# Squares of k from the third chunk on, instead of from the fourth

## The chip, the cores and the metric

The kernel runs on one core of one Trainium2 chip. The metric is the device time of one execution in microseconds (us). Several runs are made and their median is given; a profile is taken of one execution.

## The reference

A retention layer in its parallel form is followed by a feed-forward block, all in float32.

```python
# q, k, v: (8, 8, 576, 64)
scores = q @ k.T / sqrt(64)
Dmat[i, j] = gamma[h] ** (i - j) if i >= j else 0      # gamma[h] = 1 - 2 ** (-5 - h)
x = (scores * Dmat) @ v            # -> (8 * 576, 512) = (4608, 512)
h = x @ w_in                       # (512, 2048)
g = h * erf(softplus(h))
out = g @ w_out                    # (2048, 512)
```

The weights come as float64 and are rounded on the chip to float32.

## The kernel before, in words

**Pieces and chunks.** The 4608 tokens are cut into 36 pieces of 128 (`pieces`, L108). Four full pieces of batch b, four of batch b + 1, and a ninth made of the two tails of 64 tokens each; then the next two batches. So pieces 8, 17, 26 and 35 have two parts. Four pieces make a chunk (PC = 4), nine chunks the whole. Chunk 2, the third, is pieces 8 to 11.

**A piece of attention** has three steps (`stages`, L430). `transposes(i)` (L311) makes qT and kT, with the head dimension on the partitions. `scores(i)` (L337) multiplies them on TensorE (PE) into two PSUM tiles s, and VectorE (DVE) masks them into sT (L348). `outputs(i)` (L350) multiplies sT with v and qT with the state of the earlier pieces into two PSUM tiles o; for a piece of one part it also multiplies k with v (L384), for the state of the pieces behind it. DVE scales o into x, and POOL or DVE makes the new state (L423). A piece with two parts makes no state, so it does not use k by rows outside `transposes`.

**Two ways to a transpose.** By rows: `load_rows` (L136) brings q or k with the tokens on the partitions, in two loads of 128 KB (256 bytes in a row); PE transposes four times against an identity (L328) into a PSUM tile pt_q or pt_k, and ScalarE (ACT) copies it to qT or kT (L330, L334). By squares: `load_squares` (L123) brings the same numbers so that 32x32 blocks already lie where they belong; DVE then transposes inside the blocks, straight to qT or kT (L322), and PE and ACT have no part in it. Such a load is four DMAs of 112 KB for a full piece (896 bytes in a row) and eight of 48 KB for one with two parts. Squares hold each token's neighbours too, so 448 KB move instead of 256 KB. They have two buffers each (tags "qs" and "ks"); rows of k and v have four.

**Which way a piece goes.** Pieces below SQUARES = 8 go by rows. From piece 8 on q goes by squares (L153 to L156). k goes by squares from SQUARES_K = 12 on (L157); below that by rows. From 12 on, k by rows is loaded as well where the piece has one part, for L384 (L159). `transposes(i)` takes whichever is there (L317).

**Order of the work.** It is written out by hand. All DMAs that matter here are issued by SyncE (SP) in program order: `transposes(i)` ends with the loads of q, and of squares of k, of piece i + 2 (L335), and `outputs(i)` with those of k and v by rows of piece i + 3 (L426). Behind and between them SP also issues the weights (`load_weights`, L228), a second part of the constants (L733) and the stores of finished chunks of x (`store_x`, L460). The string at L723 orders the first chunk: "a" is the next step of attention, "p" four products of the first chunk of the feed-forward block, "w" a load of weights, a digit so many steps of rounding weights. Pieces 8 to 11 come behind that string, in `firsts[1].plain()` (L745, the second chunk of the feed-forward block) and in the blocks after it (from L754); their loads are issued earlier, from the end of the string on. Between these PE runs products p, pe, pg (L546) and a, e (L600). DVE rounds weights there too (L255 to L268), multiplies t by s (L569) and makes sums of w_out and w_in (L204, L214).

Of the kernel before, what the change touches and what calls it, by code (L numbers as in the profile page):

```python
# [54 lines left out]
def kernel(  # L55
# [45 lines left out]
    def flat(ap):  # L101
        return ap.rearrange("p h d -> p (h d)")
# [5 lines left out]
    pieces = []  # L108
# [3 lines left out]
    PC = TCH // P  # L112
# [4 lines left out]


    SQUARES = 2 * PC
    SQUARES_K = 3 * PC  # L120
    SQ = 32

    def load_squares(i, name, src):  # L123
        t = raw.tile([P, NP, P * D // SQ], FP32, tag=name + "s", name=f"raw_{name}s", bufs=2)
        for b, s0, n, r0 in pieces[i]:
            m = n // SQ * D
            for part in range(P // SQ):
                e, d0 = part // 2, part % 2 * SQ
                tokens = src[b, e * NP : (e + 1) * NP, s0 : s0 + n, :].rearrange("p (r a) d -> r p (a d)", r=SQ)
                at = r0 // SQ * D  # L130
                nc.sync.dma_start(  # L131
                    out=t[part * SQ : (part + 1) * SQ, :, at : at + m - SQ], in_=tokens[:, :, d0 : d0 + m - SQ]
                )
        return t

    def load_rows(i, name, src, bufs):  # L136
        if name == "q":
            t = raw.tile([P, NP, P * D // SQ], FP32, tag="qs", name="raw_q", bufs=bufs)
            t = t.rearrange("p a x -> p (a x)")[:, : H * D].rearrange("p (h d) -> p h d", h=H)
        else:  # L140
            t = raw.tile([P, H, D], FP32, tag=name, name=f"raw_{name}", bufs=bufs)
        for b, s0, n, r0 in pieces[i]:
            for e in range(2):
                heads = src[b, e * NP : (e + 1) * NP, s0 : s0 + n, :]
                nc.sync.dma_start(out=t[r0 : r0 + n, e::2, :], in_=heads.rearrange("h p d -> p h d"))  # L145
        return t

    def load(i, names="qkv"):
        if i < len(pieces):
            t = loaded.setdefault(i, {})  # L150
            for name in names:
                src = {"q": q, "k": k, "v": v}[name]
                if name == "q" and i < SQUARES:  # L153
                    t["q"] = load_rows(i, "q", q, 2)
                elif name == "q":
                    t["qs"] = load_squares(i, "q", q)  # L156
                    if i >= SQUARES_K:  # L157
                        t["ks"] = load_squares(i, "k", k)
                elif name == "v" or i < SQUARES_K or len(pieces[i]) == 1:  # L159
                    t[name] = load_rows(i, name, src, 4)  # L160

    load(0)
    cst = cpool.tile([P, CONST_COLS], FP32, name="cst")
    nc.sync.dma_start(out=cst[:, :CONST_FIRST], in_=consts[:, :CONST_FIRST])
# [4 lines left out]
    gq, gq2 = (g.rearrange("p (a i) -> p a i", a=NP) for g in (gq, gq2))  # L169
    gp = gp.unsqueeze(2).to_broadcast([P, NP, D])  # L170
    load(1)


# [128 lines left out]
    def weigh_values(i):  # L302


        if i < len(pieces) and i not in weighed:
            weighed.add(i)
            t = (loaded.get(i) or live[i])["v"]
            by = gk if len(pieces[i]) == 1 else gk2
            nc.gpsimd.tensor_tensor(out=t, in0=t, in1=by.unsqueeze(2).to_broadcast([P, H, D]), op=ALU.mult)

    def transposes(i):  # L311
        t = live[i] = loaded.pop(i)
        if i < SQUARES:
            weigh_values(i)
        for name in "qk":
            tT = t[name + "T"] = att.tile([P, NP, P], FP32, tag=name + "T", name=name + "T")
            if name + "s" in t:  # L317
                for _, _, n, r0 in pieces[i]:
                    a = r0 // SQ * D
                    squares = t[name + "s"][:, :, a : a + n // SQ * D].rearrange("p h (a d) -> p h a d", d=D)  # L320
                    order = "p h (a r) -> p h a r" if name == "q" else "p h (r a) -> p h a r"
                    nc.vector.transpose(  # L322
                        out=tT[:, :, r0 : r0 + n].rearrange(order, r=SQ), in_=squares[:, :, :, :SQ]
                    )
            else:
                pt = ps_at.tile([P, NP, P], FP32, tag="at", name=f"pt_{name}")
                for p in range(NP):
                    nc.tensor.transpose(pt[:, p, :], flat(t[name][:, 2 * p : 2 * p + 2, :]), ident)  # L328
                if name == "q":
                    nc.scalar.copy(  # L330
                        out=tT.rearrange("p h (a r) -> p h a r", r=SQ), in_=pt.rearrange("p h (r a) -> p h a r", r=SQ)
                    )
                else:
                    nc.scalar.copy(out=tT, in_=pt)  # L334
        load(i + 2, "q")  # L335
# [14 lines left out]
    def outputs(i):  # L350
# [76 lines left out]
        if i + 1 >= SQUARES:  # L427
            weigh_values(i + 1)

    stages = [(transposes, 0), (scores, 0)]  # L430
    for i in range(len(pieces)):
        stages += [(transposes, i + 1), (outputs, i), (scores, i + 1)]
        if i in (PC + 1, 2 * PC - 1):
            stages[-3:-1] = stages[-2], stages[-3]
# [397 lines left out]
```

## Time and profile before

| | |
|---|---|
| median of 3 runs | 1027.74 us (1027.37 to 1028.41) |
| the profiled execution's own time | 1027.74 us |
| its span | 1026.0 us |
| PE busy | 1017.5 us, 99% |
| DVE busy | 669.1 us, 65% |
| ACT busy | 390.4 us, 38% |
| POOL busy | 123.7 us, 12% |
| DMA | 165.76 MB, mean 162 GB/s |
| granted clock of TensorE | 0.999 |

The span runs from the first to the last instruction of the profiled execution; its own time is measured around it. "Busy" is the time in which an engine has at least one instruction running. A timeline line gives the start, the duration of the merged group, engine, line, operation, what is written from what, partitions and sizes, and the number of instructions merged. Buffer numbers are left out, so kT is the kT of any piece. SPq stands for SP's queue of instructions, which issues DMAs; a DMA lands some time after its issue. Pieces are told apart by their order in time: in the profile PE starts the scores of piece 8 at 64.77 us, of 9 at 73.84, of 10 at 82.44 and of 11 at 92.64.

### The profile page before, as it was taken

Reading aid. Unit: us, or ns where it says so; the run is one execution under the profiler, and the core shown is the slowest. Engines: PE = TensorE matmul, PEld = TensorE weight load, DVE = VectorE, ACT = ScalarE, POOL = GpSimd, SP = SyncE. Lnnn points to the kernel's source line nnn. Section 1 sums busy time; section 2 is a strip of 40 time slices with the busy share of each in tenths; the row PEclk is TensorE's granted clock in tenths of the full one; section 3 lists DMA queues with packets and bytes.
Section 4 is the critical chain, followed back from the end, with each engine's and each line's share of the span. In section 5 each row is a group of like instructions: output and inputs, shape, how many; then the busy total and the mean of one; then the engine's idle time right before and its main releaser. Section 6 shows DMA issues by size and latency. Waiting matters only on the chain.

```text
span 1026.0 us, 15946 instructions
## 1 busy us (share of the span) xinstructions
PE 1017.5 (99%) x6346; PEld 876.1 (85%) x6346; DVE 669.1 (65%) x1054; ACT 390.4 (38%) x481; POOL 123.7 (12%) x122
## 2 busy tenths in 40 slices
PE   9999999999999999999999999999999999999998
PEld 8778888888888888888888888888888888888887
DVE  3868777877976656656666666666567655555555
ACT  2254134233234444434343444444433333333332
POOL 2143112122312110010001001000100000000000
PEclk9999999999999999999999999999999999999999
DMA  9999889979984344544444345444333334444333
GB/s 197 191 241 194 224 194 221 251 155 248 242 187 161 120 150 145 168 158 163 156 150 163 123 146 160 167 144 144 144 124 124 123 131 126 131 136 133 124 91 115
DMA packets 146986, 165.76 MB, mean 162 GB/s; under 512 B 97376, under 2 KB 121568, under 8 KB 138848
## 3 DMA queue, kind: packets, MB, share of 16 engines
q1 hardware_dynamic: 145904, 163.96, 56.5%
q8 instruction: 50, 0.82, 0.3%
q10 hardware_dynamic: 1008, 0.79, 0.3%
q14 instruction: 24, 0.20, 0.1%
HBM read 117.52 MB, written 47.19 MB: 161 GB/s over the span
## 4 chain that ended last, share of the span: by engine, by line
PE 89%; DMA 5%; DVE 3%; SPq 3%; issue 1%; POOL 0%; DVEq 0%; POOLq 0%
PE a L600 23%; PE a L492 22%; PE g L600 11%; PE g L492 11%; PE e L600 6%; PE e L492 5%; PE s L343 3%; PE o L361 2%; DMA raw_qs<-in_q_dram 1%; PE p L546 1%; SPq L145 1%; PE o L384 1%; PE o L372 1%; DMA raw_k<-in_k_dram 1%; SPq L131 1%; DMA raw_ks<-in_k_dram 1%
## 5 line engine op out<-in xcount | busy, mean ns | idle before, releaser
L492 PE MATMUL a<-x,wa 128*128 128x256 f32 x1088 | 258.3, 380 | 0.0
L492 PEld LDWEIGHTS a<-x,wa 128*128 128x128 f32 x1088 | 205.7, 190 | 28.5
L600 PE MATMUL a<-wb,s 128*128 128x256 f32 x864 | 205.7, 381 | 0.0
L600 PEld LDWEIGHTS a<-wb,s 128*128 128x128 f32 x864 | 162.9, 190 | 23.6 <-ACT o L614 0.7
L99 DVE TENSOR_TENSOR t<-g,t 128x512 f32<-128x512 f32 x68 | 46.9, 690 | 150.3 <-ACT t L522 113.1
L492 PE MATMUL g<-x,wa 128*128 128x256 f32 x544 | 129.2, 380 | 0.0
L492 PEld LDWEIGHTS g<-x,wa 128*128 128x128 f32 x544 | 102.8, 190 | 14.4
L99 DVE TENSOR_TENSOR o<-a,o 128x512 f32<-128x512 f32 x108 | 74.2, 687 | 49.3 <-PE a L600 49.3
L517 ACT COPY t<-a 128x512 f32<-128x512 f32 x34 | 19.9, 586 | 188.2 <-PE a L492 188.2
L99 DVE TENSOR_TENSOR t<-t,s 128x1024 f32<-128x1024 f32 x72 | 89.6, 1285 | 0.0
L561 ACT ACTIVATE s<-t 128x1024 f32<-128x1024 f32 x72 | 72.1, 1049 | 27.8 <-DVE t L99 27.8
L270 POOL TENSOR_TENSOR wraw<-wraw 128x512 f32<-128x512 f32 x28 | 29.5, 1053 | 435.6 <-DVE wraw L268 178.9
L99 DVE TENSOR_TENSOR x<-x 128x512 f32<-128x512 f32 x115 | 75.8, 692 | 1.2
L528 ACT COPY t<-a 128x512 f32<-128x512 f32 x34 | 19.9, 587 | 144.4 <-PE a L492 144.4
L565 ACT ACTIVATE s<-s 128x1024 f32<-128x1024 f32 x72 | 72.1, 1049 | 0.4
L600 PE MATMUL g<-wb,s 128*128 128x256 f32 x288 | 68.6, 381 | 0.0
L600 PE MATMUL e<-wb,t 128*128 128x256 f32 x288 | 68.5, 380 | 0.0
L600 PE MATMUL a<-wb,t 128*128 128x256 f32 x288 | 68.5, 380 | 0.0
L600 PE MATMUL g<-wb,t 128*128 128x256 f32 x288 | 68.2, 380 | 0.0
L99 DVE TENSOR_TENSOR sT<-s,cst 128x512 f32<-128x512 f32 x72 | 46.2, 682 | 32.5 <-PE s L343 32.5
L99 DVE TENSOR_TENSOR o<-g,o 128x512 f32<-128x512 f32 x72 | 49.3, 684 | 24.6 <-ACT o L614 19.8
L492 PE MATMUL e<-x,wa 128*128 128x256 f32 x272 | 64.8, 381 | 0.0
(75 smaller groups left out, 1226.2 us busy)
## 6 DMA issues: line engine op xcount, KB each, us to landing
od<-o SPq DMA_DIRECT2D x54, 512.0 KB, 3.3
x<-xd SPq DMA_DIRECT2D x27, 1024.0 KB, 4.8
o<-od SPq DMA_DIRECT2D x27, 1024.0 KB, 5.2
raw_qs<-in_q_dram SPq DMA_DIRECT2D x96, 112.0 KB, 4.4
raw_ks<-in_k_dram SPq DMA_DIRECT2D x84, 112.0 KB, 4.1
xd<-x SPq DMA_DIRECT2D x9, 1024.0 KB, 5.3
raw_k<-in_k_dram SPq DMA_DIRECT2D x64, 128.0 KB, 4.5
raw_v<-in_v_dram SPq DMA_DIRECT2D x64, 128.0 KB, 4.5
```

The source lines that it names most:

```text
L99: nc.vector.tensor_tensor(out=out, in0=in0, in1=in1, op=op)
L131: nc.sync.dma_start(out=t[part * SQ : (part + 1) * SQ, :, at : at + m - SQ], in_=tokens[:, :, d0 : d0 + m - SQ])
L145: nc.sync.dma_start(out=t[r0 : r0 + n, e::2, :], in_=heads.rearrange("h p d -> p h d"))
L270: engine.tensor_tensor(out=r_f, in0=high_f, in1=r_f, op=ALU.mult)
L343: nc.tensor.matmul(ps[e][:, p, :], lhsT=t["kT"][heads[e], p, :], rhs=t["qT"][heads[e], p, :], start=True, stop=True)
L361: nc.tensor.matmul(o[p % 2][heads[(e + p) % 2], p // 2, :], lhsT=t["v"][:, 2 * p + e, :], rhs=t["sT"][:, e, p, :], start=(p < 2), stop=(no ...
L492: nc.tensor.matmul(acc[:, j * TH : (j + 1) * TH], lhsT=weights["wa", self.g][:, a, d, j * P : (j + 1) * P], rhs=x[self.g, self.c][a][:, d, :],
L517: nc.scalar.copy(out=self.t1[:, 1], in_=self.a)
L528: nc.scalar.copy(out=self.t2[:, 0], in_=self.a)
L561: nc.scalar.activation(self.s[:, j], t, AF.Softplus)
L565: nc.scalar.activation(self.s[:, j], self.s[:, j], AF.Erf)
L600: nc.tensor.matmul(acc[:, tp, :], lhsT=left[:, j * TH + tp * P : j * TH + (tp + 1) * P], rhs=weights["wb", self.g][:, b, j, :], start=(sta ...
```

## The change

k goes by squares from piece 8 on, as q does, in place of from piece 12 on. SQUARES_K is gone.

```diff
     SQUARES = 2 * PC
-    SQUARES_K = 3 * PC
     SQ = 32
...
                     t["qs"] = load_squares(i, "q", q)
-                    if i >= SQUARES_K:
-                        t["ks"] = load_squares(i, "k", k)
-                elif name == "v" or i < SQUARES_K or len(pieces[i]) == 1:
+                    t["ks"] = load_squares(i, "k", k)
+                elif name == "v" or len(pieces[i]) == 1:
                     t[name] = load_rows(i, name, src, 4)
...
-            if name + "s" in t:
+            if i >= SQUARES:
```

The last edit selects the same branch as before. In the order of instructions on each engine, PE loses four groups of four transposes pt_k, ACT four copies kT, DVE gets kT right behind qT for pieces 8 (two halves), 9, 10 and 11. On SP the four loads of k by rows of piece 8 (64 KB each) go; eight loads of squares of k for piece 8 and four each for pieces 9, 10 and 11 come in, each right behind the loads of q of its piece. All else keeps its order.

## Prediction

> **What bounds the kernel now.** The profiled execution took 1027.74 us, the same as the median of the three runs (1027.37 to 1028.41); its span is 1026.0 us and 1.74 us lie around it. All sums below are made against these 1027.74 us. I read the busy slices of the page first.
>
> ```profile
> PE   9999999999999999999999999999999999999998
> DVE  3868777877976656656666666666567655555555
> DMA  9999889979984344544444345444333334444333
> ```
>
> TensorE (PE) is busy throughout, so whatever PE no longer does is time saved if its inputs still come in time. But in the first 300 us, the attention part, the DMA engines are as full as PE. The change lies there: pieces 8 to 11 (62 to 98 us). Next the table by stretches; columns are PE, weight loads, DVE, ACT, POOL, granted PE clock, DMA share, GB/s.
>
> ```profile
> 54.00:62.00 8.00, 7.03 (x117) 5.43 (x116) 4.95 (x11) 7.94 (x10) 4.53 (x5) 1.00 0.66 156
> 62.00:70.00 8.00, 7.88 (x52) 6.39 (x50) 5.20 (x11) 4.19 (x8) 4.31 (x5) 1.00 1.18 292
> 70.00:80.00 10.00, 10.00 (x112) 8.15 (x112) 8.16 (x14) 1.55 (x3) 2.88 (x3) 1.00 1.12 283
> 80.00:90.00 10.00, 10.00 (x100) 8.23 (x94) 8.75 (x16) 5.31 (x8) 3.66 (x3) 1.00 0.93 190
> 100.00:110.00 10.00, 10.00 (x95) 8.16 (x94) 9.93 (x15) 1.17 (x2) 2.06 (x2) 1.00 0.90 251
> 130.00:140.00 10.00, 10.00 (x95) 8.16 (x94) 4.82 (x8) 6.23 (x7) 1.61 (x2) 1.00 0.55 134
> ```
>
> From 62 to 80 us the DMA share is over 1 (packets overlap in an engine): transfers are saturated exactly where the change adds some. DVE has about 2 us of idle time in 10 there, and none from 100 to 110.
>
> **What goes from PE.** Four groups pt_k, each of four transposes (L328). Their price is the distance between starts in PE's timeline:
>
> ```profile
> 62.51 0.60 PE L328 MATMUL pt_k<-ident,raw_k 128*128 128x128 f32 x4
> 62.95 1.03 PE L546 MATMUL p<-x,wa 128*128 128x256 f32 x4
> ...
> 66.83 1.03 PE L546 MATMUL p<-x,wa 128*128 128x256 f32 x4
> 67.98 0.63 PE L328 MATMUL pt_k<-ident,raw_k 128*128 128x128 f32 x4
> 68.44 1.03 PE L546 MATMUL p<-x,wa 128*128 128x256 f32 x4
> ...
> 76.76 0.60 PE L328 MATMUL pt_k<-ident,raw_k 128*128 128x128 f32 x4
> 77.20 1.03 PE L546 MATMUL pg<-x,wa 128*128 128x256 f32 x4
> ...
> 82.44 1.16 PE L343 MATMUL s<-qT,kT 64*128 64x128 f32 x16
> ```
>
> A group costs 0.44 us (62.51 to 62.95; 76.76 to 77.20; likewise 86.22 to 86.66). The second costs more: 66.83 to 68.44 is 1.61, where a plain group of four lasts 0.86 (77.20 to 78.06), so 0.75. Sum: 3 x 0.44 + 0.75 = 2.07 us, all on the chain that ends last, since PE has no gap here. ACT loses four copies kT of 0.59 us; ACT is not on the path, so I count nothing. pt_k also gives up its turn in the four PSUM tiles that it shares with s and o; o of piece 10 then needs the tiles of o of piece 9, which DVE has read by 82.3 today, 6 us before o starts at 88.48: nothing, and if DVE is 4 us late still nothing.
>
> **What DVE gets.** kT by 32x32 blocks. Pieces 12 and later already do it: 1110 ns for one piece, 404 ns for each half of a two-part piece like piece 8. So 2 x 0.40 + 3 x 1.11 = 4.1 us more. DVE was idle from 63.16 to 65.96 (between qT of piece 8 and its sT), 73.23 to 75.03, and 83.0 to 84.19; these gaps hide the work if its data are there. If they are not, DVE waits in order, and all queued behind waits too: roundings of w_out, the products t*s (3.2 us), x, sT.
>
> **What the queues get.** On SP piece 8 trades 4 row loads of k (64 KB each) for 8 square loads (48 KB each); pieces 9 to 11 keep k's rows, which the state needs (L384), and add four square loads of 112 KB each. That is 16 more issues, all ahead of what follows in SP's order; above all, xd's stores and the loads of pieces 9 to 12 come after more work. In SP's order the squares of k of piece 10 come right behind the squares of q of piece 10. So when did those land?
>
> ```profile
> 71.34 6.22 SPq L131 DMA_DIRECT2D raw_qs<-in_q_dram  x8
> ...
> 79.53 0.71 DVE L322 STREAM_TRANSPOSE qT<-raw_qs 128x512 f32<-128x512 f32 x1
> ```
>
> The eight are pieces 10 and 11. The fourth, the last of piece 10, is issued at 74.5; the DMA view of that moment alone (kind, size, us to landing) shows
>
> ```profile
> raw_qs<-in_q_dram SPq DMA_DIRECT2D x1, 112.0 KB, 4.9
> ```
>
> so q of piece 10 is there at 79.4, and DVE takes it at 79.53: 3 us ahead of the scores at 82.44. That is the tight place. In the changed kernel eight more loads (k of 9, k of 10) go through the saturated engines before k of 10 is complete. Price, from a stretch with almost nothing but such packets of 896 B (76 to 78 us):
>
> ```profile
> DMA packets 537, 0.44 MB, mean 221 GB/s; under 512 B 60, under 2 KB 535, under 8 KB 535
> q1 hardware_dynamic: 537, 0.44, 115.3%
> ```
>
> 512 packets (4 loads, 0.459 MB) take 2.08 us at 221 GB/s; eight take 4.2. Bounds: 3.2 at the 283 to 292 GB/s that the saturated stretches show with larger transfers mixed in, and 4.8 at 0.6 us for a load (the eight loads of q took 6.22 us to issue, 0.78 each, with a pause in it). I take 4.2, since that row has the same packets. The exchange at piece 8 shifts what follows: SP saves 3.4 us (47.29 to 50.67) and spends 8 x 0.47, so +0.4; with waiting for older loads I take 0.5, bounds 0 and 1.5 (DMA is only at 0.66 there). Piece 8 itself: its squares of k land near 62.7, DVE finishes kT near 64.0, scores want it at 64.3; I count nothing, at worst 1 us.
>
> A rule speaks for a cheaper load. The Trainium skill, "DMA: Bandwidth & Descriptors", section "Specifications", gives 512 B as the size from which transfers reach line rate, and about 358 GB/s as the limit to HBM; 896 B would then be as good as any. The trace disagrees: 221 GB/s at 76 to 78 us with the share at 1.15, and 220 GB/s at 80 to 82 us where 1494 of 1556 packets are below 512 B. By the rule the eight loads would be an estimated 2.6 us instead of 4.2, and the result 1.6 us lower.
>
> **The sum.** Squares of k of piece 10 complete at 79.4 + 0.5 + 4.2 = 84.1. kT takes 1.11, so scores of piece 10 start at 85.25. PE, which has saved 0.44 + 0.75 + 0.44 = 1.63 by then, would be ready at 82.44 - 1.63 = 80.81: a new wait of 4.4 us. Then 2.07 saved against 4.4 waited: +2.4. DVE leaves the wait some 4 us late with sT of piece 10 behind two roundings, x, the state and w_out's sums; from its rows sT ends near 91.0 where PE wants it at 90.9, and sT of piece 11 about as close, so I add 0.3 (bounds 0 and 2). Together +2.7: **1030.4 us**. After 88 us SP waits for buffers again (gaps at 87.7, 94.6, 103.0) and the DMA share falls to 0.55 by 130 to 140 us, so the backlog drains and does not come back. Pieces 12 and later load what they loaded before.
>
> **Rivals.**
> 1. *Faster: the loads are hidden.* PE gaps stay zero and the 2.07 us arrive: 1025.7. It decides at 79.7: if k of piece 10 is complete by 80.81 - 1.11, PE does not wait. For it: the loads are issued two pieces ahead, into two buffers. Against: even q alone lands at 79.4 today, and eight loads would have to cost nothing.
> 2. *About even: the loads overlap better.* If they land at 82.0 (2.6 us later than q now), the wait is 82.0 + 1.16 - 80.81 = 2.35 against 2.07: 1028.0. For it: single engines look free within the saturated share, since packets overlap.
> 3. *Much slower: the wait spreads.* Piece 8 or 9 also comes late, the loads cost 4.8, the shift 1.5, and DVE, 99% busy from 100 to 110 us, cannot catch up, so sT or x of pieces 10 to 12 is late each time. With 79.4 + 1.5 + 4.8 + 1.16 - 80.81 - 2.07 = +4.0 and 1.5 behind it: 1033.2.
>
> That the edit does nothing is excluded: the new instruction order has 16 fewer PE transposes, 4 fewer ACT copies, 5 more DVE transposes and 16 more loads.
>
> **How the numbers follow.** A difference of 0.2% (2.06 us) is about what a measurement of this kernel can tell from no change. The forecast (1028.9 to 1032) has 0.56, of it 0.50 beyond 2.06 us and 0.06 within. Rival 1 has 0.17, of it 0.13 as faster (2.07 lies just on the edge; a little less waiting elsewhere decides) and 0.04 within. Rival 2 has 0.12, within. Rival 3 has 0.15, slower. So faster 0.13, same 0.22, slower 0.65. The range runs from 1025.5, the full saving, to 1034.0, which takes in most of rival 3.
>
> **What would show it.** Right: scores s of piece 10 on PE start about 3 us later than 82.44, behind kT, and kT behind raw_ks; the distance from s of piece 8 to s of piece 9 is shorter by 0.75; PE then keeps its pace, and from 140 us all is shifted by one amount. Wrong: no idle time of DVE in front of kT, or s of piece 10 at about 80.8 (rival 1); a second and third wait on kT or sT between 90 and 115 us (rival 3). If the squares of k of piece 10 are complete before 81, my price of a load in a saturated stretch is what failed.

## The result, and the profile after

| | before | after |
|---|---|---|
| median | 1028.08 us (1027.37 to 1028.72, 4 runs) | 1033.97 us (1033.50 to 1037.60, 4 runs) |
| the profiled execution | 1027.74 us | 1033.80 us |
| its span | 1026.0 us | 1032.0 us |
| PE busy / DVE busy | 1017.5 / 669.1 us | 1017.5 / 672.3 us |

The ratio after to before is 1.0065, with a 95% interval of 1.0041 to 1.0089: the changed kernel is slower, by 5.9 us in the medians and by 6.06 us between the two profiled executions. (The ratio is that of the means, which the one run of 1037.60 us pulls up; the medians give 1.0057.) The forecast was +2.7.

PE's busy time is the same, though PE has four groups of transposes less. Most of what the groups saved was spent again elsewhere at a slower clock, as will be seen. The busy slices of the page after:

```profile
PE   9998999999999999999999999999999999999998
DVE  3868877877877566666666666666657655555555
DMA  9989989979984444444445334444433334444433
```

PE's fourth slice (77 to 103 us) has fallen from 9 to 8. It is the only visible change on PE's line. The table by stretches says it better (columns as in the table of before: PE, weight loads, DVE, ACT, POOL, granted PE clock, DMA share, GB/s):

```profile
54.00:62.00 8.00, 7.03 (x118) 5.42 (x117) 5.09 (x12) 7.66 (x10) 4.09 (x5) 1.00 0.43 88
62.00:70.00 8.00, 8.00 (x63) 6.48 (x61) 4.30 (x11) 3.27 (x5) 3.21 (x4) 1.00 1.13 248
70.00:80.00 10.00, 9.67 (x108) 7.92 (x107) 8.23 (x12) 0.59 (x1) 4.06 (x3) 1.00 1.03 303
80.00:90.00 10.00, 5.68 (x31) 4.67 (x30) 7.15 (x14) 1.53 (x3) 3.09 (x3) 0.83 1.21 210
...
130.00:140.00 10.00, 10.00 (x99) 8.12 (x96) 6.22 (x12) 5.98 (x7) 1.93 (x3) 1.00 0.58 117
```

Three numbers matter. From 80 to 90 us PE is busy for only 5.68 us. In the same stretch its clock is 0.83 instead of 1.00. And from 54 to 62 us, ahead of everything else, the DMA share is 0.43 at 88 GB/s, where it was 0.66 at 156: the changed kernel moves fewer bytes there, not more. PE's timeline shows the wait itself:

```profile
80.51 1.03 PE L544 MATMUL pe<-x,wa 128*128 128x256 f32 x4
85.86 2.08 PE L341 MATMUL s<-qT,kT 64*128 64x128 f32 x16 [4.32 <-DVE kT L320]
87.86 1.74 PE L544 MATMUL pg<-x,wa 128*128 128x256 f32 x4
89.44 1.89 PE L598 MATMUL a<-wb,t 128*128 128x256 f32 x8
```

The scores of piece 10 start at 85.86 instead of 82.44, after 4.32 us in which PE waited for kT. DVE's timeline hands the question on to the DMA:

```profile
82.43 0.71 DVE L320 STREAM_TRANSPOSE qT<-raw_qs 128x512 f32<-128x512 f32 x1
84.62 1.09 DVE L320 STREAM_TRANSPOSE kT<-raw_ks 128x512 f32<-128x512 f32 x1 [1.48 <-DMA raw_ks<-in_k_dram]
```

The last of piece 10's squares of k landed at 84.50; those of q at 82.31 (79.41 before).

One smaller loss lies ahead of it. The store of the first chunk of x went 2.8 us later than before (67.75 instead of 64.99) and landed at 75.63 instead of 71.52. DVE could not write x before that, and sT of piece 9 stood behind x:

```profile
75.72 0.76 DVE L99 TENSOR_TENSOR x<-o,cst 128x256 f32<-128x256 f32 x2 [1.77 <-DMA xd<-x]
```

So PE lost 0.8 us at o of piece 9 before it came to the wait at piece 10. Behind the wait at piece 10 the clock shows itself, microsecond by microsecond:

```profile
85.00:86.00 1.00, 0.14 (x2) 0.17 (x3) 1.00 (x2) 0.00 (x0) 0.00 (x0) 0.86 1.16 206
86.00:87.00 1.00, 1.00 (x10) 1.00 (x12) 0.97 (x4) 0.00 (x0) 0.17 (x1) 0.50 1.17 204
...
88.00:89.00 1.00, 1.00 (x3) 0.82 (x4) 0.41 (x1) 0.00 (x0) 1.00 (x1) 0.50 1.35 214
89.00:90.00 1.00, 1.00 (x6) 0.90 (x5) 0.41 (x1) 0.36 (x1) 1.00 (x2) 0.93 1.36 222
```

PE starts again at half speed: s takes 2.0 us to the next group's start where it took 1.09, pg 1.58 where it took 0.96. And much later, far from the change, a second wait has grown:

```profile
237.88 1.10 DVE L320 STREAM_TRANSPOSE kT<-raw_ks 128x512 f32<-128x512 f32 x1 [2.49 <-DMA raw_ks<-in_k_dram]
```

Before, the same kT waited 1.09 us for its squares and PE not at all; now PE waits 1.15 us for it.

**Where the 6.06 us are**, by the start of the same PE instruction in both profiles: the changed kernel is 1.77 us ahead at 75 us; 0.97 ahead at the products after o of piece 9; 3.42 behind at the scores of piece 10; 4.95 behind at a (89.44), the clock having cost 1.53; 4.51 after the last transposes saved; 5.73 behind at the scores at 239.13; 6.08 at those at 278.09, and from there on.

### The profile page after: what moved, and what is told of

Read it like the earlier page. It is cut to its first block, busy times and chain, and to the rows that moved or that the text cites. A ratio compares the mean times of both kernels' runs of the same rounds, so it can differ in the third digit from the quotient of the medians.

```text
span 1032.0 us, 15934 instructions
## 1 busy us (share of the span) xinstructions
PE 1017.5 (99%) x6330; PEld 876.1 (85%) x6330; DVE 672.3 (65%) x1059; ACT 388.3 (38%) x477; POOL 124.2 (12%) x122
## 4 chain that ended last, share of the span: by engine, by line
PE 90%; DMA 5%; DVE 3%; SPq 1%; ACT 1%; issue 1%; POOL 0%; DVEq 0%; POOLq 0%
PE a L598 23%; PE a L490 22%; PE g L598 11%; PE g L490 11%; PE e L598 6%; PE e L490 5%; PE s L341 3%; PE o L359 3%; DMA raw_ks<-in_k_dram 2%; PE o L382 1%; PE o L370 1%; DMA raw_qs<-in_q_dram 1%; DMA xd<-x 1%; SPq L130 1%; PE idle L704 1%; DVE t L99 1%
```

## The experiments

Each kernel has its own runs of before on the same chip beside it (median 1027.98 to 1028.63 us), and its ratio, of means, is to those. There is one profile of each kernel. Three theories stood at the start. **A**: one wait at the scores of piece 10, the cold clock behind it, and a rest of the loads' backlog. **B**: the volume of the added loads costs 6 us wherever it lies. **C**: DVE's added transposes are what costs.

| kernel | median, us | ratio to before, interval |
|---|---|---|
| volume alone, behind piece 11 | 1028.90 | 1.0008 [0.9998, 1.0017] |
| changed, squares of 9 to 11 not loaded | 1029.99 | 1.0019 [1.0010, 1.0028] |
| the same without DVE's transposes for them | 1028.36 | 1.0001 [0.9990, 1.0011] |
| PE's saving alone (9 to 11) | 1027.47 | 0.9990 [0.9981, 0.9998] |
| changed, 14 products in the wait | 1034.30 | 1.0055 [1.0041, 1.0068] |
| changed, 18 products in the wait | 1035.11 | 1.0065 [1.0053, 1.0078] |
| changed, store of x moved back | 1035.09 | 1.0075 [1.0061, 1.0088] |
| changed, squares of k on ACT's queue | 1037.14 | 1.0089 [1.0075, 1.0103] |
| changed, squares of k of 9 first | 1034.85 | 1.0059 [1.0046, 1.0071] |
| piece 8 alone by squares | 1029.99 | 1.0021 [1.0012, 1.0030] |
| changed, piece 8 by rows | 1030.73 | 1.0021 [1.0013, 1.0030] |
| changed, half the squares of k of 8 | 1031.15 | 1.0031 [1.0019, 1.0043] |
| 9 and 11 alone by squares | 1028.10 | 1.0003 [0.9994, 1.0012] |
| 11 alone by squares | 1027.74 | 0.9991 [0.9982, 1.0000] |

### The volume by itself

```diff
+            if i == 11 and "v" in names:
+                for j in range(2):
+                    load_squares(i, "k", k)
```

> The kernel before with two pieces' squares of k (8 loads of 112 KB, 0.92 MB) loaded behind the rows of piece 11 and never used; all arithmetic is that of before. Theory A (one wait: the 6 us come from PE waiting for the squares of k of piece 10, from its clock at half speed after that wait, and from a rest of the backlog): these loads stand ahead of nothing that is needed within 10 us, so no wait near 80 to 100 us; PE is at most 0.3 us later at 120 us, and the whole takes 1028 to 1029. Theory B (volume: the whole attention part is as much bound by DMA as by PE, and 1.5 MB more cost 6 us wherever they stand): 0.92 MB cost 3.7 us, 1031.7.

Measured +0.9 us. At 98 us PE is where it was in before (92.52 instead of 92.64 at the scores of piece 11); what is lost is lost at the scores at 233 and 272 us. 0.92 MB of transfers that nobody waits for cost under 1 us, so B falls. A keeps its place, though the late loss is not explained by it.

### The changed kernel without the volume of pieces 9 to 11

```diff
-                    t["ks"] = load_squares(i, "k", k)
+                    if SQUARES < i < SQUARES + 4:
+                        t["ks"] = shared[0]
+                    else:
+                        t["ks"] = load_squares(i, "k", k)
+                        shared.append(t["ks"])
```

> The changed kernel, but pieces 9 to 11 take the squares of k of piece 8, and theirs are not loaded (so the scores of these three pieces are those of other keys). PE, ACT and DVE do exactly the work of the changed kernel; 1.34 MB of loads are gone. Theories A and B both: no wait at the scores of piece 10, the 2.07 us of PE are saved, 1026. Theory C (the 4.1 us more on DVE are what is too much): still slower than before, over 1030.

Measured +2.0 us, 1030 instead of the 1026 that A and B expected. 4 of the 6 us go with these loads, but PE's saving does not appear. PE's timeline:

```profile
81.66 1.16 PE L346 MATMUL s<-qT,kT 64*128 64x128 f32 x16 [0.70 <-DVE kT L325]
...
87.63 1.64 PE L364 MATMUL o<-sT,raw_v 128*64 128x128 f32 x16 [0.29 <-issue]
```

PE waits for kT at piece 10 and then for sT: o lasts 1.64 us instead of 1.09 because the second half of sT is late. From 66.8 us to its wait for POOL at 85.4 DVE stands idle for 0.29 us only, and the transposes of kT (1.06 to 1.08 us each) stand in that chain. So C may hold a part.

### The same without DVE's transposes

```diff
+            if name == "k" and SQUARES < i < SQUARES + 4:
+                t["kT"] = shared[-1]
+                continue
```

> The changed kernel, but kT of pieces 9 to 11 is that of piece 8: neither their squares of k are loaded (1.34 MB) nor does DVE transpose them (3 x 1.1 us); the scores of these three pieces are of other keys. What stays of the change is PE's saving of 2.07 us. Theory A with DVE as a second bound (shown by the run without the volume, where DVE's transposes ate the saving): PE is 1.6 to 2.1 us ahead of the kernel before at 98 us and the time is 1025.9 to 1027. If something else than DVE's transposes ate it, PE is less than 1 us ahead at 98 us and the time 1027.5 to 1029, as without the volume.

Measured 1028.36 us: 1.6 us less than with the transposes (ratio 1.0001 instead of 1.0019), which is DVE's part by the medians, but still no gain over before, where 1026 to 1027 was expected. The two profiles show less of DVE's part: PE is 0.3 us apart in them at 101 us and 0.7 us at the end. Something else of the change ate PE's saving. PE's timeline names it:

```profile
81.63 1.16 PE L350 MATMUL s<-qT,kT 64*128 64x128 f32 x16 [0.93 <-DVE qT L329]
```

Now the scores wait for **qT**. The squares of q, which the change leaves alone, landed at 80.65 us instead of 79.41. The only loads that this kernel has more than before are those of piece 8, and they delay what SP issues behind them: DVE waited 1.09 us for the squares of q of piece 9 and 0.92 us for the first store of x, and for neither of them before.

### PE's saving alone

Before, with kT of pieces 9 to 11 that of piece 8: no group pt_k for them, no load and no DVE work added.

```diff
+            if name == "k" and SQUARES < i < SQUARES_K:
+                t["kT"] = shared[-1]
+                continue
```

> The kernel before, but kT of pieces 9 to 11 is that of piece 8, made from rows as before: three groups of transposes fewer on PE and three copies on ACT, no load and no DVE instruction added; the scores of these three pieces are of other keys. It is the run without DVE's transposes, less the exchange at piece 8. PE's saving is 0.75 + 2 x 0.44 = 1.63 us. If the exchange ate the saving there, this run shows it: PE 1.4 to 1.7 us ahead at 98 us, time 1026.2 to 1027. If DVE's chain from qT of piece 10 to sT of piece 10 (79.5 to 86.9 us in the kernel before) or q's squares of piece 10 (there at 79.4) hold PE, it is under 0.9 us ahead at 98 us, time 1027.3 to 1028.3.

Measured 1027.47 us, 1.2 us below its runs of before. In its profile PE goes from 0.74 us behind before (lost ahead of 40 us) to 0.89 ahead: all of the expected 1.63 us, with no wait at the scores of piece 10. It then gives back 0.3 us at 272 us. So the saving is real, and neither DVE's old chain nor q's squares hold it back. The kernel above differs from this one in the exchange at piece 8 alone (which saves it 0.44 us more on PE and gives DVE two half transposes), so that is where its saving went.

### Piece 8 alone

```diff
-                    if i >= SQUARES_K:
+                    if i >= SQUARES_K or i == 8:
                         t["ks"] = load_squares(i, "k", k)
-                elif name == "v" or i < SQUARES_K or len(pieces[i]) == 1:
+                elif name == "v" or i < SQUARES_K and i != 8 or len(pieces[i]) == 1:
```

> The kernel before with k by squares for piece 8 alone (a piece of two parts, which needs no rows of k elsewhere): on SP eight loads of 48 KB instead of four of 64 KB (+0.13 MB), on PE one group of transposes less (0.44 us), on DVE two half transposes (0.8 us) in its idle time at 63 to 66 us. Theory A: no new wait, 0.3 to 0.5 us faster, 1027.3 to 1027.8. Theory B by volume (0.13 of 1.5 MB): +0.5 us, 1028.5. If the exchange delays q of piece 10, up to 1029.

Measured +1.9 us (1029.99 against 1028.07), where A expected a small gain. PE's timeline:

```profile
67.21 1.03 PE L547 MATMUL p<-x,wa 128*128 128x256 f32 x4
70.88 0.63 PE L329 MATMUL pt_k<-ident,raw_k 128*128 128x128 f32 x4 [2.65 <-DMA raw_k<-in_k_dram]
```

The transposes of piece 9, which nobody touched, wait 2.65 us for rows of k. On SP these stand behind the squares of q of piece 9, and those were issued at 63.19 instead of 60.97. The 0.13 MB more are an estimated 0.6 us at the 221 GB/s of the full stretch; bytes alone do not cost 2 us here.

### The changed kernel with piece 8 by rows

> The changed kernel with piece 8 left by rows (k by squares for 9, 10 and 11 alone): SP keeps four loads of 64 KB there instead of eight of 48 KB. If the exchange at piece 8 costs about 2 us by itself (as the run with piece 8 alone showed) and the terms add up, the time is about 1032, the loads of piece 9 start 0.5 to 2 us earlier and the scores of piece 10 start at 84 to 85. If the bytes of pieces 9 to 11 alone set the end of the wait, the scores of piece 10 start at 85 to 86 and the time is 1033.5 to 1034.5 (0.44 of PE's saving less).

Measured 1030.73 us, 2.1 us above its runs of before, where the changed kernel is 5.9 above its own: leaving out the exchange at piece 8 takes away 3.8 of the 6 us (3.2 between the two medians as they stand), more than either expectation had. SP's own timeline for this kernel (start, duration of the group, line, what is loaded, number of DMAs):

```profile
54.02 1.97 SPq L132 DMA_DIRECT2D raw_qs<-in_q_dram  x4
56.09 0.38 SPq L234 DMA_DIRECT2D wraw<-in_moe_w_out_dram  x1
56.51 0.43 SPq L734 DMA_DIRECT2D cst<-in_decays_dram  x1
57.03 2.50 SPq L132 DMA_DIRECT2D raw_qs<-in_q_dram  x4
```

and for the changed kernel:

```profile
53.60 1.64 SPq L130 DMA_DIRECT2D raw_qs<-in_q_dram  x3
55.28 5.13 SPq L130 DMA_DIRECT2D raw_ks<-in_k_dram  x8
60.51 0.38 SPq L231 DMA_DIRECT2D wraw<-in_moe_w_out_dram  x1
60.93 0.43 SPq L731 DMA_DIRECT2D cst<-in_decays_dram  x1
61.46 1.80 SPq L130 DMA_DIRECT2D raw_qs<-in_q_dram  x4
```

The eight small loads of piece 8 hold SP from 55.28 to 60.41. Sixteen loads of 48 KB in a row (eight of q, eight of k) carry too little: seven of these eight take SP 0.43 us each and start 0.47 us apart, 48 KB in 0.47 us is about 105 GB/s, and the DMA engines stand half idle meanwhile. Everything behind them comes later. (The fourth of the eight took 1.80 us. An issue of 1.0 to 1.9 us stands between 56 and 59 us in 13 of the other kernels too, so it is not the exchange's; its cause is not shown.) For this kernel the stretch reads

```profile
54.00:62.00 8.00, 7.03 (x118) 5.42 (x117) 4.89 (x11) 7.67 (x9) 4.08 (x5) 1.00 0.90 227
```

a share of 0.90 against the changed kernel's 0.43. The wait at the scores of piece 10 shrinks from 4.32 to 1.16 us, and they start at 82.53. This profile is of a run 1.4 us below its median, so the medians carry the size and the profile the mechanism.

### Half the squares of k of piece 8

```diff
-        for b, s0, n, r0 in pieces[i]:
+        for b, s0, n, r0 in pieces[i][: 1 if name == "k" and i == SQUARES else 2]:
...
-                    a = r0 // SQ * D
+                    a = 0 if name == "k" and i == SQUARES else r0 // SQ * D
```

> The changed kernel, but of the squares of k of piece 8 only the first part's four loads are issued (48 KB each), and both halves of kT are made from them: scores of the second tail are of other keys. DVE and PE do the same as in the changed kernel; SP has four issues fewer (4 x 0.47 = 1.9 us) and 0.19 MB less. If SP's issue time is what the exchange costs, the constants and the squares of q of piece 9 are issued about 2 us earlier (59 instead of 61 us), the scores of piece 10 start 2 us earlier (83.9) and the time falls by 2 to 3.5 us to 1030.5 to 1032. If it is the bytes alone (0.19 of 1.5 MB) or DVE's halves, it falls by less than 1 us: 1033 to 1034.

Measured 1031.15 us, 2.8 us less than the changed kernel. PE and DVE do what they do there; four loads of 48 KB fewer are issued. Its SP timeline:

```profile
55.17 1.86 SPq L130 DMA_DIRECT2D raw_ks<-in_k_dram  x4
57.13 0.38 SPq L231 DMA_DIRECT2D wraw<-in_moe_w_out_dram  x1
57.55 1.35 SPq L731 DMA_DIRECT2D cst<-in_decays_dram  x1
```

The constants go at 57.55 instead of 60.93. The scores of piece 10 start at 82.82, after 1.73 us of waiting. 0.19 MB at the rate of the full stretch (221 GB/s) is 0.9 us; four issues of 0.47 us are 1.9. Bytes alone do not give 2.8, nor does DVE, whose work is unchanged. What fits is SP's time at a place where what stands behind it has to be out before the full stretch. That time is more than the 1.9 us of the issues: part of it is SP's waiting for older loads, as the section on the prediction shows.

### Bytes moved into the hole

The squares of k of piece 9 are issued ahead of q of piece 8, where the DMA engines have room.

> The changed kernel with the squares of k of piece 9 issued ahead of the squares of q of piece 8 instead of behind those of q of piece 9: same bytes, but 0.46 MB go while the DMA share is 0.3 to 0.7 (52 to 62 us) instead of into the full stretch from 64 us on. Theory 'position' (what counts is bytes in the full stretch): q and k of piece 10 land about 2 us earlier, the scores of piece 10 start at about 84, perhaps 0.5 us are lost at piece 8, whose squares come later; time 1031.5 to 1033. Theory 'issue' (SP's 0.47 us for each issue ahead of piece 9 counts, wherever it is put): piece 8 is 1 to 2 us late, the loads of piece 9 start as late as in the changed kernel, time 1034 to 1036.

Measured 1034.85 us, no gain, which is the reading by issues, though PE loses only 0.53 us at piece 8 and not 1 to 2. The squares of q of piece 9 go at 63.06 instead of 61.46, and the squares of k of piece 10 land at 83.88, only 0.6 us earlier. Room on the DMA engines did not help where SP could not fill it.

### Another queue for the squares of k

> The changed kernel with the squares of k of pieces 8 to 11 issued on ACT's queue instead of SP's; same bytes. Rival 'window' (SP has 8 loads in the air at a time, and each takes 4.3 us, so a further queue brings more at once): the squares of k of piece 10 land at least 2 us earlier than 84.5 us, the scores of piece 10 start between 83.0 and 84.3 because DVE arrives at about 82.4, and the time falls by 1.5 to 3 us to 1031 to 1032.5. Rival 'engines' (the DMA engines are full, the queue does not matter): squares of k land within 1 us of 84.5, time 1033 to 1034.5. If ACT is itself late with its issues, squares come later and the time is above 1034.5.

Measured 1037.14 us, outside both expectations but for the last sentence. ACT's own work stood behind its issues: eight of them kept it from 47.96 to 53.57, four more from 57.64 to 61.47, and DVE and PE waited for ACT's share of the roundings:

```profile
63.20 0.43 DVE L253 TENSOR_SCALAR wb<-wb 128x512 f32<-128x512 f32 x1 [3.36 <-ACT wb L248]
```

What a free queue would bring stays open.

### The store of x behind the loads

```diff
-    store_x(1)
...
+    store_x(1)
     for b, nxt in zip(blocks[2:], blocks[3:] + [None]):
```

> The changed kernel with the store of the second chunk of x (1 MB) issued behind the loads of pieces 10 to 12 and not ahead of them. Same bytes. Theory A: squares of k of piece 10 are complete 2.6 us earlier, near 81.9; PE waits 1.8 us in place of 4.3 and stays at full clock; 4.1 us are won there, so 1028.4 if the backlog is gone by 240 us, and up to 1030 if its rest shows again. Theory B: the same bytes cost the same; the waits move to between 180 and 280 us, 1033.9.

Measured 1035.09 us, no gain. The scores of piece 10 start at 85.83 as in the changed kernel: the squares of k land at 84.40, and DVE, late from earlier waits, takes qT only at 83.66. Two causes end there together, so taking away one shows nothing. This profile is also of the slowest of the five runs, 2.9 us above their median, and its loads were late before the store's place: its constants, the load on SP that follows those of piece 8, went at 62.68 and not at 60.93. What the store's place is worth stays open.

### The clock

```diff
+        if i == 10:
+            for _ in range(14):
+                nc.tensor.matmul(ps[0][:, 0, :], lhsT=ident, rhs=ident, start=True, stop=True)
```

> The changed kernel with 14 extra products of the identity with itself (about 3.1 us) in PE's order just ahead of the scores of piece 10, into the same PSUM tile, overwritten by the scores. Theory A: PE still waits until about 85.8 us, but idles for only about 1.2 us, so its clock stays at full speed; scores and the products behind them take 1.09 + 0.96 us in place of 2.0 + 1.58; PE is 1.5 us earlier at 92 us, and the whole is 0.5 to 1.5 us shorter, 1032.4 to 1033.4. Theory B: PE gains 1.5 at 92 us, but the wait for squares of k near 239 us grows by as much; 1033.9.

Measured 1034.30 us. The products ended at 84.83 and the squares of k landed later in that run (85.71), so PE still stood for 2.15 us, and the clock fell all the same:

```profile
87.00:88.00 1.00, 1.00 (x14) 1.00 (x16) 0.97 (x3) 0.00 (x0) 0.00 (x0) 0.77 1.12 193
88.00:89.00 1.00, 1.00 (x7) 0.77 (x6) 1.00 (x4) 0.00 (x0) 0.96 (x1) 0.50 1.29 202
```

This run says nothing on the price. With 18 products the rest of the wait was 1.24 us:

> The changed kernel with 18 further products ident x ident on PE (about 0.235 us each, 4.2 us in all, as in the run with 14) ahead of the scores of piece 10, into a tile s that the scores then overwrite. They fill PE's idle time there, so that PE stands still for at most 1.2 us. Theory A (one wait, and behind it about 1.5 us because the granted clock falls to 0.50 after the idle time): the clock from 85 to 92 us stays near 1.00, s takes 1.1 instead of 2.0 us and the pg behind it 0.96 instead of 1.58; PE is 1.0 to 1.5 us earlier than in the changed kernel at 98 us; the time falls by 0.5 to 1.5 us to 1032.5 to 1033.5, less where the later waits on squares of k at 239 and 278 us grow in turn. Theory B (the volume alone costs 6 us, wherever): the same time as the changed kernel, 1034. If the dummies overrun the wait, PE is late by what they overrun.

```profile
87.00:88.00 1.00, 1.00 (x16) 0.97 (x16) 0.96 (x3) 0.00 (x0) 0.00 (x0) 1.00 1.08 190
88.00:89.00 1.00, 1.00 (x8) 0.83 (x5) 1.00 (x4) 0.00 (x0) 0.94 (x1) 1.00 1.31 206
```

The clock stays at 1.00, and the time is 1035.11 us, not lower. PE's timeline shows why:

```profile
87.00 1.16 PE L344 MATMUL s<-qT,kT 64*128 64x128 f32 x16 [1.24 <-DVE kT L320]
...
93.05 1.64 PE L362 MATMUL o<-sT,raw_v 128*64 128x128 f32 x16 [0.37 <-issue]
```

The scores start 1.1 us later than in the changed kernel, because the squares of k landed 1.2 us later (85.73), though nothing about the loads was changed; and o then waits for sT and is stretched. Between the scores of piece 10 and o of piece 11 the run loses 1.31 us more against before (from 4.56 behind to 5.43, with 0.44 saved between), where the changed kernel lost 1.53 to the clock. In the changed kernel the slow clock hid DVE's lateness; with the clock kept, DVE takes nearly the same. So A's term is real in the profile, but holding the clock did not bring its size back.

### Two smaller versions

`i in (9, 11)` and `i == 11` in place of the test for piece 8 above.

> The kernel before with k by squares for pieces 9 and 11 alone: PE saves 0.75 + 0.44 = 1.19 us, DVE gets two transposes of 1.1 us, SP eight loads of 112 KB more, none for pieces 8 and 10. Four loads fewer lie ahead of q of piece 11 and none behind q of piece 10, so the scores of piece 10 wait for qT at most 0.3 us. Expected -1.19 + 0.5 for later squares and o: 1027.3 to 1028.2, no difference to the kernel before or up to 1 us faster. If the four loads of piece 9 delay q of piece 10 by 2 us, the scores of piece 10 wait 1 us: 1028.5 to 1029.5.

> The kernel before with k by squares for piece 11 alone: one group of transposes less on PE (0.44 us), one transpose of 1.1 us more on DVE at about 95 us, 0.46 MB more in the loads, behind those of piece 10. By half of what the run with 0.92 MB of unused squares showed (+0.9 us) this is -0.44 + 0.45: 1027.5 to 1028.5, no difference. If DVE's chain at 93 to 99 us is the tight one, o of piece 11 waits up to 1 us: 1028.5 to 1029.3.

Measured 1028.10 and 1027.74 us, ratios 1.0003 [0.9994, 1.0012] and 0.9991 [0.9982, 1.0000], as expected. PE was 0.86 and 0.77 us ahead of before at 86 us; the first had given back 0.9 by 233 us and was 0.18 ahead in the end, the second gave back 0.5 by 272 us. Both are faster than the changed kernel by about 6 us; neither can be told from the kernel before.

## Why the prediction was right and wrong

The direction, the place and the wait were right. The sum was short by 3.4 us, in two terms behind the wait and one ahead of it.

**Right: the place and the mechanism.** The scores of piece 10 wait for kT and kT for its squares of k, complete at 84.50 where 84.1 was predicted; the scores start at 85.86 (85.25), the wait is 4.32 us (4.4). The distance from the scores of piece 8 to those of piece 9 shrank by 0.75 us (64.19 to 72.51), as foreseen. The four loads of piece 10's k took 2.19 us from 82.31 to 84.50, 209 GB/s, so the price taken from the trace (221 GB/s) held. The rule that 512 B reach line rate at up to 358 GB/s (the Trainium skill, "DMA: Bandwidth & Descriptors", section "Specifications") did not.

**In part luck: how well the numbers of the wait agree.** PE came to it 0.7 us later than foreseen, because of o of piece 9, and the loads came 0.6 us later, so the length of the wait agrees. And 84.50 is one run's number: in the kernels with 14 and 18 products, whose loads are those of the changed kernel, the squares of k landed at 85.71 and 85.73.

**Wrong: what follows the wait, "so I add 0.3 (bounds 0 and 2)".** Measured 1.53. The text had DVE's lateness in it and no clock. Either of the two is enough: 1.53 with the slow clock, 1.31 without.

**Wrong: "the backlog drains and does not come back".** The DMA share did fall to 0.58 from 130 to 140 us. But the squares of k at 237.88 were late again, and 1.57 us were lost from 233 to 278 us. How much of this belongs to the change is open: in all kernels tried PE lost 0.2 us or more there against before's profile, also in the one with nothing added to the loads (0.3 with PE's saving alone).

These two and the 0.6 us by which the scores came later than predicted make 1.2 + 1.6 + 0.6 = 3.4 us, the difference between +2.7 and +6.06.

**Wrong, and hidden in the profile: the exchange at piece 8, "I take 0.5, bounds 0 and 1.5".** In medians it costs 1.9 us alone and 3.8 within the change, each against its own runs of before. The part that failed is "waiting for older loads", to which 0.1 us was left. The 3.4 us that SP saves were counted rightly: SP comes to the squares of q of piece 8 at 53.6 us on average in the six kernels with piece 8 by rows, and at 50.2 in the seven that have all eight loads of k in their place. But from there to the constants it takes 11.3 us instead of 5.3, so the eight loads cost 6.0 us and not 3.8. In 2.4 of the 11.3 us SP stands until the DMA eight issues ahead has landed, mostly a load of weights, against 0.3 of the 5.3 us: SP comes earlier, but that load does not. So the constants go at 61.5 on average instead of 58.9.

The profile of before could not show this: its constants went at 60.18, the latest of the six (the others 56.51 to 59.95). Against it the changed kernel's 60.93 looks like +0.75; against the mean it is +2.0. Nor does this cost stand beside the 3.4 us above; it is another cut through the same 6 us. Without the exchange the wait itself shrinks from 4.32 to 1.16 us, and the clock does not fall.

**The rivals.** That the loads are hidden or overlap better fell with the wait of 4.32 us. "The wait spreads" (1033.2) came nearest in size, and piece 9 did come late, by 0.8 us at its o. But pieces 10 and 11 show no further wait of PE in the profile after: the clock had slowed PE to about DVE's pace, as the run with 18 products showed.

**What is not settled**: how the 0.2 to 1.7 us at 233 to 278 us come about (in the kernels with ACT's queue and with the store moved back PE lost 4.8 and 5.7 us behind 188 us), and why the exchange costs more together with the other loads (3.8) than alone (1.9).

## What to carry to other kernels

A trade of few large loads for many small ones is priced by the issuing queue's time where that queue is the limit, its waits for older loads included, and by bytes only where the DMA engines are full: look at the DMA share of the stretch in which the new issues stand. An instruction stream that is late by chance in one profile, with slack, hides what is added to it, so a shift of the loads is read from several runs. And a wait of some microseconds on PE can be followed by a term of its own, a slower clock or the late engine behind it; here the two ran side by side and did not add up.

## What the runs showed of the hardware

- PE's clock fell to 0.50 after idle times of 4.32, 3.58, 2.86, 2.40, 2.15 and 2.12 us, and did not after 3.31, 2.65, 2.11, 1.73, 1.24 and 1.16 us. What decides is where the gap lies. In the clock records of all 16 traces each stretch between two changes of the clock is a whole multiple of 3.41 us, so they give a grid of steps of 3.41 us in each run, and each of these falls lasted one step. The clock fell after every step in which PE had stood idle for 2.12 us or more, and after none with 1.96 or less. The gap of 3.31 us (squares of k on ACT's queue) lay across two steps, 1.72 and 1.60 us, and cost no clock; that of 2.15 us (14 products) lay within one. The Trainium skill, "TensorE: Matmul & The Clock Gate", section "Part 1: The HAM clock gate", states half clock after at least one idle window of about 3.4 us that runs freely, and full clock after one busy window. The step of 3.41 us agrees; that the window must be idle throughout does not, for 2.12 us of it were enough.
- SP has at most eight DMAs on their way. In all 16 traces no DMA of SP's (11,252 issues) started before the one eight issues ahead had landed. The fourth load of piece 10's squares of k was issued at 80.21, right after the store of x eight issues ahead of it landed at 80.19; in the kernel with piece 8 by rows it was 76.80 after 76.78. A store of 1 MB that takes 6 to 8 us, as the first store of x did in every trace (6.17 to 7.89), is thus a place in the queue lost for that long.
